# Fewer tiling changes in a fused attention and MoE kernel: three score units per visit, sums in one PSUM bank, pieces in the freed score slots

## Chip, cores and metric

One core of one Trainium2 chip. The metric is the device time of one execution in microseconds (us), the median of several. A profile's span is some 1.8 us shorter than the time of the same execution (338.66 against 336.9 for the kernel before). A run is called slow when it is over 1.5% above the fastest of its kernel; ratios use fast runs alone.

## The reference

```python
def _attn_ref(q, k, v):                 # (8, 12, 448, 64): batch, heads, sequence, head size
    scores = scale * np.matmul(q, k.transpose(0, 1, 3, 2))
    m = np.max(scores, axis=-1, keepdims=True)
    e = np.exp(scores - m)
    attn = e / (np.sum(e, axis=-1, keepdims=True) + np.exp(-m) + 1e-09)
    return np.matmul(attn, v)

def _moe_ref(x, w1, w2, w3, w_out):     # x (3584, 768); all weights (768, 768)
    h = np.maximum(np.maximum(x @ w1, x @ w2), x @ w3)
    return h @ w_out
# x is the attention's output as (8*448, 12*64)
```

## The kernel before

The work comes in 24 groups (a batch and two pairs of heads). A group has seven **score units** (four corners of 64x64 tiles, 448 columns each; they fill a two-bank PSUM slot of which three exist) and two **sums** (exponentials times v, one per pair of heads: 26 small 64x64 matmuls and 18 wide 128x128 ones). Between them TensorE does **pieces** of the projections: "up" pieces of six 448-column matmuls and "out" pieces of six 384-column ones, each in one of two further PSUM banks. A **visit** is a stretch in which TensorE leaves the pieces, changes to 64x64 tiles for scores and small sums, and comes back.

```python
visits = ((0, 1), (2, 3), (4, 5, 6))            # three visits for each group
for i in range(3, NI):
    ...
    for vi, units in enumerate(visits):
        scores(i, ej, units)                     # slots of ps_s (3 x 2 banks), exponentials on ScalarE
        if vi < 2:
            finish = av(i - 1, pj, vi, ...)      # sums of the group before, also in a slot of ps_s
        ...
        fill(per)                                # pieces, in banks of ps_b (2 x 1 bank)

def av(i, ej, pr, part):
    if i >= LAST:                                # from group 6 on
        av_tail(i, ej, pr, (0, 1, 2))            # 12 small sums, row tile r in bank r
        av_last(i, ej, pr)                       # 14 small sums of the last window
        return av_main(i, ej, pr, (0, 1, 2), True)   # 18 wide sums, then VectorE, ScalarE

def up_piece(b, fcs, i, q0, qn):
    p_i = ps_b.tile([128, 512], FP32, tag="b", name="p_i")
    # 6 matmuls with xT[b], then VectorE: hT = max(hT, p_i)

# the last tile's stores, out of add_out
cuts = [(0, NW, (sy, sy)), (NW, 256, (sc, sc)), (NW + 256, 128, (sy, sc))]
```

The softmax here doesn't subtract the row's maximum and nothing guards it: scores larger than these inputs give would overflow.

## Time and profile before

| | kernel before |
|---|---|
| time, median of 3 | 338.64 us (338.59 to 338.93) |
| span of the profile | 336.9 us |
| last matmul starts, by the trace | 331.38 us |
| tail, from there to the end | 5.50 us |
| normal visit of two units with sums | 1.394 us |

The prediction below reads the busy table, the chain, the waits and a timeline. Two more views: first the groups of instructions (line, engine, operation, out<-in, shapes, count | busy us, mean ns of one | idle before it and who ended that):

```profile
L490 PE MATMUL p_i<-xT,w 128*128 128x448 f16 (+2 forms) x972 | 173.1, 332 | 0.5 <-DMA xT<-xn 0.3
L324 ACT ACTIVATE e<-stp 128x896 f16<-128x896 f32 (+4 forms) x171 | 143.9, 901 | 60.3 <-PE stp L304 60.1
```

The pieces (L490) are half of the span and hardly ever wait. The exponentials (L324) are long, 0.9 us each, but ScalarE is idle 60 us for want of scores: here nobody on TensorE waits for it. Then the end of the timeline (start us, length us, engine, line, operation; SPq and ACTq are the sequencers of SyncE and ScalarE that issue DMAs):

```profile
330.10 3.88 SPq L531 DMA_DIRECT2D out_dram<-o_sb  x5
330.29 1.31 PE L514 MATMUL op_ps<-w,hT 128*128 128x256 f16 x12
...
331.60 1.84 ACTq L531 DMA_DIRECT2D out_dram<-o_sb  x3
```

The last store is issued on SyncE until 333.98, 2.6 us after the last matmul's start; the change tries to shorten that.

### The profile page before, as it was taken

The numbers are of one execution on the slowest core, as the hardware profiler recorded it, in microseconds if no ns is written. First come the engines' busy times: TensorE is split into PE (matmuls) and PEld (weight loads), VectorE is DVE, ScalarE is ACT, GpSimd is POOL, SyncE is SP. The second block draws the span as 40 slices with busy tenths as digits, with TensorE's granted clock in tenths as the row PEclk, the third lists the DMA queues.
The fourth block names the chain that finished last, engine by engine and source line by source line (L and its number), as shares of the span: only waits on it lengthen the run. The fifth ranks groups of instructions, "written<-read, shape, count | busy, mean of one in ns | idle before, by whom it ended". The sixth has DMA issues, their size and how long they took to land.

```text
span 336.9 us, 10248 instructions
## 1 busy us (share of the span) xinstructions
PE 326.1 (97%) x4316; PEld 195.9 (58%) x4316; DVE 199.9 (59%) x521; ACT 183.1 (54%) x289; POOL 146.7 (44%) x260
## 2 busy tenths in 40 slices
PE   7899999999999999999999999999999999999993
PEld 3668788866556655565546646555556555565552
DVE  4556675566566556556656556556556556575552
ACT  4768856655665755676556655666565665420000
POOL 8596578880671539170854328351754000000000
PEclk9999999999999999999999999999999999999999
DMA  8999999799799999969996999989990730124016
GB/s 141 197 200 207 203 205 191 128 161 191 109 108 132 171 234 145 124 96 190 177 156 81 114 259 120 150 99 220 186 149 18 164 89 2 31 47 129 0 33 157
DMA packets 84815, 46.46 MB, mean 138 GB/s; under 512 B 53280, under 2 KB 81312, under 8 KB 84768
## 3 DMA queue, kind: packets, MB, share of 16 engines
q0 software_dynamic: 29120, 21.80, 48.6%
q1 hardware_dynamic: 55264, 23.60, 41.3%
q8 instruction: 34, 0.56, 0.7%
q10 hardware_dynamic: 384, 0.39, 0.4%
q14 instruction: 13, 0.11, 0.1%
HBM read 44.04 MB, written 11.01 MB: 163 GB/s over the span
## 4 chain that ended last, share of the span: by engine, by line
PE 87%; DMA 5%; ACT 2%; DVE 2%; issue 1%; POOL 1%; POOLq 0%; ACTq 0%
PE p_i L490 48%; PE op_ps L514 14%; PE stp L304 11%; PE avp L388 9%; DMA xT<-xn 3%; ACT e L324 2%; DMA ld_q<-in_q_dram 2%; PE avp L344 2%; PE avp L361 1%; DVE xn L404 1%; PE trT L229 1%; DVE QT L190 1%; PE xtp L463 0%; ACT QT L188 0%; DVE rb L401 0%
## 5 line engine op out<-in xcount | busy, mean ns | idle before, releaser
L324 ACT ACTIVATE e<-stp 128x896 f16<-128x896 f32 (+4 forms) x171 | 143.9, 901 | 60.3 <-PE stp L304 60.1
L490 PE MATMUL p_i<-xT,w 128*128 128x448 f16 (+2 forms) x972 | 173.1, 332 | 0.5 <-DMA xT<-xn 0.3
L490 PEld LDWEIGHTS <-w 128*128 128x128 f16 x972 | 90.2, 98 | 69.1 <-issue 6.0
L249 POOL COPY QT<-QT 64x384 f16<-64x384 f16 (+1 forms) x84 | 46.9, 558 | 93.9 <-DMA QT<-ld_q 69.2
L501 DVE TENSOR_TENSOR hT<-hT,p_i 128x448 f16<-128x448 f16 (+2 forms) x96 | 59.7, 622 | 35.7 <-PE p_i L490 35.6
L514 PE MATMUL op_ps<-w,hT 128*128 128x384 f16 (+2 forms) x342 | 58.5, 323 | 0.0
L304 PE MATMUL stp<-QT,KT 64*64 64x448 f16 (+2 forms) x756 | 48.1, 338 | 2.6 <-ACT e L324 0.9
L499 DVE CAST hT<-p_i 128x448 f16<-128x448 f32 (+2 forms) x48 | 30.0, 625 | 25.2 <-PE p_i L490 25.2
L514 PEld LDWEIGHTS <-hT 128*128 128x128 f16 x342 | 32.0, 98 | 22.4 <-issue 2.0
L424 ACT ACTIVATE xn<-end,rl 64x64 f16<-64x64 f32 x72 | 24.9, 346 | 34.5 <-DVE rl L421 34.1
L521 DVE TENSOR_SCALAR o_sb<-op_ps 128x384 f32<-128x384 f32 (+2 forms) x57 | 31.2, 547 | 17.4 <-PE op_ps L514 16.8
L388 PE MATMUL avp<-vx,e 128*128 128x65 f16 x936 | 38.6, 194 | 0.0
L388 PEld LDWEIGHTS <-e 128*128 128x128 f16 x936 | 32.1, 97 | 2.3
L304 PEld LDWEIGHTS <-KT 64*64 64x64 f16 x756 | 15.8, 105 | 26.8 <-issue 23.9
L398 DVE TENSOR_SCALAR rb<-avp 128x6 f32<-128x6 f32 (+2 forms) x54 | 8.8, 164 | 36.8 <-PE avp L388 36.8
L404 DVE TENSOR_TENSOR xn<-avp,rb 128x384 f16<-128x384 f32 (+2 forms) x54 | 29.3, 543 | 1.8
L433 POOL COPY vx<-ld_v 128x768 f16<-128x768 f16 x21 | 17.2, 820 | 6.8 <-issue 4.2
L344 PEld LDWEIGHTS <-e 64*64 64x64 f16 x624 | 13.7, 107 | 8.1 <-issue 1.7
L102 POOL DMA_DIRECT2D ld_q<-in_q_dram x24 | 17.4, 723 | 2.3 <-DMA w<-in_moe_w_dram 1.1
L102 POOL DMA_DIRECT2D ld_k<-in_k_dram x24 | 17.3, 722 | 2.1 <-DMA w<-in_moe_w_out_dram 1.1
L414 ACT ACTIVATE end<-avp 128x65 f32<-128x65 f32 x36 | 8.2, 227 | 17.1 <-PE p_i L490 12.4
L115 POOL DMA_DIRECT2D ld_v<-in_v_dram x24 | 15.2, 634 | 2.6 <-DMA w<-in_moe_w_dram 1.3
(52 smaller groups left out, 162.1 us busy)
## 6 DMA issues: line engine op xcount, KB each, us to landing
out_dram<-o_sb SPq DMA_DIRECT2D x54, 192.0 KB, 4.0
ld_v<-in_v_dram POOLq DMA_DIRECT2D x48, 128.0 KB, 5.1
ld_k<-in_k_dram POOLq DMA_DIRECT2D x23, 224.0 KB, 6.6
ld_q<-in_q_dram POOLq DMA_DIRECT2D x23, 224.0 KB, 7.5
w<-in_moe_w_dram POOLq DMA_DIRECT2D x9, 384.0 KB, 9.2
w<-in_moe_w_out_dram POOLq DMA_DIRECT2D x3, 384.0 KB, 8.5
xT<-xn SPq DMA_TRANSPOSE x18, 4.8
QT<-ld_q SPq DMA_TRANSPOSE x17, 7.3
```

The source lines that it names most:

```text
L102: nc.gpsimd.dma_start(out=tiles[nm][:, 1 : NP * T + 1].rearrange("x (r t) d -> x r (t d)", r=NP)[:, p0:p1], in_=src[:, p0:p1],)
L249: eng.tensor_copy(out=t[d0 : d0 + HP, o * 128 : (o + n) * 128], in_=t[s0 : s0 + HP, a * 128 : (a + n) * 128],)
L304: nc.tensor.matmul(out=stp[half * HP : half * HP + HP, par, j * qn : (j + 1) * qn], lhsT=k_block(i, pr, h2, x[half]), rhs=q_cols(i, pr, h2 ...
L324: nc.scalar.activation(out=dst, in_=src, func=AF.Exp, scale=scale)
L388: nc.tensor.matmul(out=ps[:, hh, j * D1 : (j + 1) * D1], lhsT=eF[:, o : o + 128], rhs=vx[:, 2 * pr + hh, (x[0]), 0:D1], start=False, stop= ...
L404: nc.vector.tensor_tensor(out=xn[i][:, pr, ws[0] : ws[0] + nw].rearrange("p j h d -> p h j d"), in0=acc[:, :, :, 0:D], in1=rb.unsqueeze(3) ...
L424: nc.scalar.activation(out=xn[i][0:HP, pr, 3, hh], in_=end[h, 0:D], func=AF.Copy, scale=rl[h])
L490: nc.tensor.matmul(out=p_i[:, j * qn : (j + 1) * qn], lhsT=w_sb[i][:, dc, ts(fc, 128)], rhs=xT[b][:, dc, q0 : q0 + qn], start=(dc == 0), s ...
L499: nc.vector.tensor_copy(out=dst, in_=src)
L501: nc.vector.tensor_tensor(out=dst, in0=dst, in1=src, op=ALU.max)
L514: nc.tensor.matmul(out=op_ps[:, 0:w], lhsT=hT[bp][:, fc, ts(t, 128)], rhs=wout_sb[:, fc, c : c + w], start=(fc == 0), stop=(fc == NFC - 1),)
L521: nc.vector.tensor_scalar(out=o_sb[:, c : c + w], in0=op_ps[:, 0:w], scalar1=1.0 / LAMBDA, scalar2=None, op0=ALU.mult,)
```

## The change

The intent: fewer changes of tiling. From group 6 on, three groups (21 units) take seven visits of three units instead of nine visits of two or three. That needs PSUM: the sums move out of the slots into one bank that is always the same, and the pieces of a visit go into the score slots as their exponentials empty them, the last one into the other bank. The order of the corners, and a no-op on ScalarE, keep small sums of two row tiles from writing one bank at once. xT (the transposed attention output) of one group more, the last of batch 1, comes by DMA and not from TensorE. The last stores go on three queues. The core of the diff, cuts marked:

```diff
+    slots = [ps.tile([128, 2, 512], FP32, name=f"ps{j}") for j in range(3)]
+    banks = [ps.tile([128, 512], FP32, name=f"pb{j}") for j in range(2)]
 ...
+    def visit(units, pair):
 ...
+        ps = banks[0]                            # the sums, always here
 ...
+            for at in anti:
+                s0(*at)
+            turned = turn_over(smalls(diag, True))
+            for s, at in ((s0, diag), (s1, anti), (s1, diag), (s2, anti), (s2, diag)):
+                for corner in at:
+                    s(*corner)
+            smalls(anti, False, turned)
+            for _, power in qk:
+                power()                          # three exponentials on ScalarE
+            wides()
 ...
-                cuts = [(0, NW, (sy, sy)), (NW, 256, (sc, sc)), (NW + 256, 128, (sy, sc))]
+                cuts = [(0, NW, (sy, sc)), (NW, 256, (gp, gp)), (NW + 256, 128, (sy, sc))]
 ...
+    def places(cols, pair):                      # where the n pieces of this visit go
 ...
+        mid = [] if pair else [banks[0]]
+        while len(mid) < n:
+            mid.append(slots[(turn["s"] + len(mid) - (not pair)) % 3][:, 0])
+        ahead.extend(mid[: max(n - 1, 0)] + [banks[1]] * (n > 0))
 ...
+    for g in range(ONE, NI, 3):                  # ONE = 6
+        todo = [(g + n // 7, n % 7) for n in range(21)]
+        for n in range(7):
+            us = todo[3 * n : 3 * n + 3]
 ...
+            if pr == 1:
+                x_transpose_dma(pi)
```

## The prediction

> **What bounds the kernel now.** I read the page's busy table and clock row first, then the chain that ended last, then the waits of TensorE, and last a timeline of TensorE alone over three visits. The busy table:
>
> ```profile
> PE 326.1 (97%) x4316; PEld 195.9 (58%) x4316; DVE 199.9 (59%) x521; ACT 183.1 (54%) x289; POOL 146.7 (44%) x260
> PEclk9999999999999999999999999999999999999999
> ```
>
> Only TensorE (PE) is full, at full clock in every slice. Busy is not yet proof, so the chain and the waits (columns: engine and line, waited for: us in total, times, longest us):
>
> ```profile
> PE 87%; DMA 5%; ACT 2%; DVE 2%; issue 1%; POOL 1%; POOLq 0%; ACTq 0%
> ...
> PE stp L304 <- ACT e L324: 0.9, 3, 0.4
> ...
> PE p_i L490 <- DMA xT<-xn: 0.3, 1, 0.3
> ...
> PEld L304 <- issue: 23.9, 74, 0.6
> ```
>
> The chain is TensorE for 87%. It waits hardly at all for another engine: 0.9 us for exponentials (in the first 40 us) and 0.3 us for one transposed xT. What stands out is the last row: 74 times the weight loader sits idle 0.32 us before a run of scores and waits for nothing. That is a cost of changing from 128x128 to 64x64 tiles. Three visits of one group (start us, length us, engine, line):
>
> ```profile
> 149.55 0.65 PE L514 MATMUL op_ps<-w,hT 128*128 128x384 f16 x3
> 150.13 0.57 PE L304 MATMUL stp<-QT,KT 64*64 64x448 f16 x8
> 150.53 0.26 PE L344 MATMUL avp<-vt,e 64*64 64x65 f16 x12
> ...
> 150.85 0.73 PE L388 MATMUL avp<-vx,e 128*128 128x65 f16 x18
> 151.43 2.11 PE L514 MATMUL op_ps<-w,hT 128*128 128x384 f16 x12
> ...
> 154.77 3.56 PE L490 MATMUL p_i<-xT,w 128*128 128x448 f16 x18
> 158.27 0.76 PE L304 MATMUL stp<-QT,KT 64*64 64x448 f16 x12
> 158.96 0.36 PE L490 MATMUL p_i<-xT,w 128*128 128x448 f16 x1
> ```
>
> Pieces (the up and out projections) run at a fixed pitch: the 18 matmuls take 3.56 us of which the last is about 0.35, so 3.21/17 = 0.189 us each; the 384-column ones 0.162 us. The pieces are already at full rate, so time can only come out of what lies between them. I measure that as (first piece after) minus (start of the last piece before plus one pitch). A visit of two score units and sums: 149.55 + 3 x 0.162 = 150.03 to 151.43 = 1.40 us. A visit of three units without sums: 154.77 + 18 x 0.189 = 158.17 to 158.96 = 0.79 us. By the trace's start stamps, the 1.394 of a normal visit is 0.094 change of tiling, 0.40 scores (2 quads of four concurrent 64x64 matmuls, about 0.2 each), 0.32 for 26 small sums (about 31 ns per four) and the change back, and 0.575 for 18 wide sums (32 ns each). The change back alone is about 0.1: a last score quad takes 0.29 us to the next piece instead of 0.19.
>
> **What the Trainium skill says.** "TensorEngine Tiling (Array Packing)", Key Properties: changing the tiling mode drains TensorE. The trace agrees: 0.094 us in and about 0.1 us out per visit. "PSUM — Partial Sum Buffer", PSUM bank collisions: two TensorE writes from different row tiles into one bank and quadrant collide. The kernel before keeps row tile r in bank r, as that asks; no run here tests it. It explains the change's order of corners and its turn-over through ScalarE. "ScalarE: Activation LUTs", What ACT_TABLE_LOAD costs: an activation with immediates takes 186 ns + 0.833 ns per column, 93 ns of it overlapped back to back. For 896 columns that is an estimate of 932, then 839; the trace has 917 and a pitch of 0.80 to 0.81. "DMA: Bandwidth & Descriptors", Issuing engines are not separate DMA queues: another issuing engine saves only the sequencer's time. In the tail of the trace that time is real: the last SyncE issues are 0.5 to 0.9 us each, in series.
>
> **The change, part by part.**
>
> 1. Fewer visits. From group 6 on, 54 visits (and two more for the last sums) become 42 and one. Sums are also moved into visits with three units: 37 of the 42 carry sums (one pair is left for the end), 5 are scores alone. Matmul counts stay at 4316 by the built program's order, so only changes of tiling and waits can differ.
>
> 2. One visit with three units and sums, if nothing waits. The two anti corners of unit 0 start at 0.094. The 14 diagonal small sums run beside them on the other two tiles, 7 per tile at about 31 ns, to 0.315. Then unit 0's diagonal corners at 0.315, unit 1 at 0.505, unit 2 at 0.694 (pitch 0.189). The 12 anti small sums run beside the end of unit 2. Wide sums start at 0.694 + 0.29 = 0.985 and end at 1.56. So the third unit costs about 0.17 where a visit of its own would add two changes of tiling. The no-op on ScalarE is ready near 0.6, before the anti sums want it at 0.69; I count nothing for it.
>
> 3. The new wait. In 36 of the 37 visits the first piece goes into the score slot of unit 0 and must wait for its exponential (the built order has a wait on ScalarE there; in one visit the only piece goes to the bank). Unit 0 is complete only at 0.315 + 0.355 (a later quad's matmul is 0.349) = 0.67; ScalarE starts 0.052 after (before: quad ends at 0.383, exponential starts at 0.435) and needs 0.917, so 1.64; TensorE starts 0.051 after an ACT end (same in every such wait before). First piece at 1.69, not 1.56: **a wait of 0.13 us in each of 36 visits**, 4.7 us. Second and third pieces (at 2.8, 4.0; or 2.7, 3.6 for out pieces) come after exponentials that end at 2.45 and 3.25: no wait. The next visit's slots were emptied long before.
>
> 4. Sum from group 6 on. Before: 34 x 1.394 + 17 x 0.788 + group 6's three (1.485 + 1.488 + 1.246, still with PE transposes of xT) + 2 x 1.018 at the end = 67.06 us. After: 36 x 1.69 + 1.56 + 5 x 0.79 + 1.33 for the last sums alone (1.02 and 0.3 for two more changes of tiling and slower pairs of small tiles) = 67.68 us. **+0.6 us**. Without the wait it would be 63.0, or -4.1 us: the wait eats the gain.
>
> 5. Off the path. ScalarE loses 36 x (0.23 + 2 x 0.35) = 33 us, VectorE swaps four small operations for two scalings. Neither is the bound (54% and 59%), so nothing.
>
> 6. xT by DMA. Before, one transfer of 9.54 us held TensorE 0.46 us. The new lead at a batch's start is about 11 us (two visits of 5.5 and one of 1.7, less 2.3 for VectorE), the slowest issue-to-landing before was 10.2: that stall may go. Batch 1's lead is only about 8 us, as the visits there have one or two pieces: maybe 0.3. At the end, four out pieces (3.9 us) cover a transfer that takes about 4.7 from the last sum: 0.1 after the first four matmuls. Net -0.1.
>
> 7. Tail. Last matmul starts at 331.38, last SyncE issue 333.51 to 333.98, landed 335.60. With one issue of the wide cut on SyncE, one on ScalarE and the middle cut on GpSimd, SyncE's last issue is some 1.2 us earlier, but GpSimd issues take 0.63 to 0.72 each and then travel: landing near 335.1 to 335.2. -0.4 us.
>
> 338.64 + 0.6 - 0.1 - 0.4 = 338.7. The pitch of small tiles in pairs may be 30 and not 31 ns; seven of them then start unit 0's diagonal corners 7 ns sooner, 0.25 us over 36 visits. I take it off: **338.4 us**.
>
> **The rivals.** (a) The gain comes whole: the first piece finds its slot free. Then 36 x 0.13 = 4.7 less, about 334. For it: nothing in TensorE's order forces the stall but that one wait. Against it: the exponential's start and length repeat to some 2 ns in the trace before. (b) The small sums do not run beside the scores on the other tiles. All four tiles running at once before (score quads 1.6 ns apart in issue) speaks against it, but mixed lengths in flight were never seen. It would add up to 0.19 us x 37 = 7 us: 345. (c) The turn-over through ScalarE is late, because the no-op queues behind exponentials of a short visit. ScalarE needs 2.5 of 5.4 us, so only in the first three visits: below 1 us. (d) xT arrives late, as its DMA now starts nearer to the bursts of loads after a group: 1 us per late batch, up to 3.
>
> **Range and chances.** (a) to (d) put the time between 334 and 345, most weight on 337 to 340. I take 334.5 to 341.5 for 8 in 10. 2% is 6.8 us: faster needs more than the whole gain of part 4 (0.03); slower needs (b) in full (0.06); within, 0.91.
>
> **What would show it.** In the profile after: tiling changes before scores fall from 74 to about 62 (54 visits become 42); a row of TensorE pieces waiting for the exponentials of about 36 times 0.13 us (right if 3 to 6 us in all, and then ACT's share of the chain grows); visits with sums take 1.69 (if 1.56, rival a; if 1.85 or more, b or c); small sums start within 10 ns of unit 0's anti corners; pieces keep 0.189; the last landing is about 3.6 us after the last matmul, not 4.2. The prediction is wrong if scores and small sums exclude each other on the array, or if unit 0's exponential can be done by 1.5.

## The result, and the profile after

**349.78 us**, median of 4 runs (348.55 to 378.87), against 338.62 (338.24 to 338.93, 4 runs) for the kernel before: ratio 1.0318, 95% interval 1.0266 to 1.037, slower. A ratio is the mean time of one kernel's fast runs over that of the other's of the same rounds, so not quite the ratio of the medians quoted. The run of 378.87 us had a granted clock of 0.85 (its trace shows 0.85 without a change from 5.5 to 374.1 us); it was the first one, none of the later runs showed it again, and its cause is open. Its profile is not used: the profile "after" below is of a second series of the unaltered kernel, 347.67 us (346.35 to 351.82, 6 runs) against 340.01 (337.78 to 342.94, 11 runs), ratio 1.0228 [1.0165, 1.0291]: still slower, but whether by more than 2% this series leaves unclear.

The busy table and the clock row of the page after:

```profile
PE 330.5 (96%) x4316; PEld 202.8 (59%) x4316; DVE 201.6 (58%) x488; ACT 149.8 (43%) x181; POOL 147.6 (43%) x262
...
PEclk9999999999999999999999999999999999999998
```

TensorE is still the only full engine, with the same 4316 matmuls. ScalarE lost 33.3 us of work (183.1 to 149.8), as predicted, and it brought nothing, as predicted. The waits (engine and line, waited for: us in total, times, longest):

```profile
ACT e L425 <- PE ps L414: 110.2, 37, 5.6
...
PEld L414 <- issue: 14.5, 42, 0.4
...
PEld L322 <- issue: 5.9, 21, 0.7
...
PE ps L594 <- DMA xT<-xn: 1.7, 1, 1.7
```

The tiling changes before scores fell from 74 to 42 + 21 = 63 (predicted: about 62). One wait for xT is longer than before. But the row that the prediction wanted, TensorE pieces waiting some 36 times for exponentials, is not there. Nobody may conclude from this that the wait is not. A normal visit with three units and sums, in the timeline of TensorE:

```profile
92.94 0.38 PE L414 MATMUL ps<-QT,KT 64*64 64x448 f16 x2
92.94 0.31 PE L452 MATMUL pb<-vt,e 64*64 64x65 f16 x8
93.09 0.23 PE L452 MATMUL pb<-vx,e 64*64 64x65 f16 x4
93.15 0.35 PE L414 MATMUL ps<-QT,KT 64*64 64x448 f16 x2
93.16 0.19 PE L452 MATMUL pb<-vx,e 64*64 64x65 f16 x2
93.19 0.54 PE L414 MATMUL ps<-QT,KT 64*64 64x448 f16 x6
...
93.85 0.74 PE L481 MATMUL pb<-vx,e 128*128 128x65 f16 x18
94.58 3.57 PE L594 MATMUL ps<-xT,w 128*128 128x448 f16 x18
```

And in the timeline of ScalarE, same window:

```profile
93.61 2.54 ACT L425 ACTIVATE e<-ps 128x896 f16<-128x896 f32 x3 [3.74 <-PE ps L414]
```

Three exponentials take 2.54 us, each about 0.917 (the mean of L425 is 918 ns), so unit 0's ends near 93.61 + 0.917 = 94.53. The first piece (94.58) starts 0.05 later. The 18 wide sums start at 93.85 and have a pitch of 32 ns: they are issued by 93.85 + 18 x 0.032 = 94.43, which is when a piece could have started. So TensorE stands for 0.15 us. The waits view misses it because the record of a wide sum lasts 0.19 us: the last one, started near 94.39, is drawn until 94.58 and covers the gap. Stalls shorter than the record of one instruction show only in start stamps.

Adding up start stamps over the trace (what lies between the last piece's pitch and the next piece, as in the prediction) splits the span of both profiles:

| us | predicted change | before | after | change |
|---|---|---|---|---|
| first stretch of pieces ends (it starts at 22.54 and 22.32) | 0 | 23.67 | 23.45 | -0.22 |
| between pieces, before group 6 | 0 | 21.80 | 22.00 | +0.20 |
| between pieces, from group 6 | +0.35 | 67.09 | 70.98 | +3.89 |
| gaps from one piece to the next | -0.1 | 1.58 | 5.00 | +3.42 |
| tail | -0.4 | 5.50 | 7.06 | +1.56 |
| span | -0.15 | 336.88 | 345.64 | +8.76 |

(The parts sum to 8.85; 0.1 is unassigned.) Three places are wrong, and each got experiments.

### The profile page after: what moved, and what is told of

It is laid out like the page before. It is cut to its first block, busy times and chain, and to the rows that moved or that the text cites. A ratio compares the mean times of both kernels' runs of the same rounds, so it can differ in the third digit from the quotient of the medians.

```text
span 377.0 us, 10297 instructions
## 1 busy us (share of the span) xinstructions
PE 364.1 (97%) x4316; PEld 215.0 (57%) x4316; DVE 202.2 (54%) x488; ACT 150.0 (40%) x181; POOL 148.0 (39%) x262
## 4 chain that ended last, share of the span: by engine, by line
PE 94%; DVE 2%; ACT 2%; issue 1%; POOL 0%; POOLq 0%; DVEq 0%; ACTq 0%
PE ps L594 28%; PE pb L594 22%; PE pb L618 8%; PE ps L618 8%; PE ps L414 7%; PE pb L481 7%; PE pb L452 3%; PE ps L322 2%; PE ps L379 2%; ACT e L342 1%; PE pb L195 1%; PE pb L247 1%; PE ps L362 1%; DVE QT L210 0%; PE ps L231 0%
## 5 line engine op out<-in xcount | busy, mean ns | idle before, releaser
L425 ACT ACTIVATE e<-ps 128x896 f16<-128x896 f32 x126 | 106.5, 917 | 149.2 <-PE ps L414 128.3
L594 PE MATMUL ps<-xT,w 128*128 128x448 f16 x480 | 109.8, 387 | 0.2 <-ACT e L425 0.2
L594 PE MATMUL pb<-xT,w 128*128 128x448 f16 (+2 forms) x492 | 91.6, 341 | 0.7 <-DVE o_sb L625 0.6
L605 DVE TENSOR_TENSOR hT<-hT,ps 128x448 f16<-128x448 f16 x59 | 36.6, 621 | 21.6 <-PE ps L594 12.8
L342 ACT ACTIVATE e<-ps 128x896 f16<-128x896 f32 (+4 forms) x45 | 36.5, 869 | 21.0 <-PE ps L322 19.3
L414 PE MATMUL ps<-QT,KT 64*64 64x448 f16 x504 | 44.0, 382 | 0.0
L618 PE MATMUL pb<-w,hT 128*128 128x384 f16 (+2 forms) x180 | 36.6, 350 | 0.0
L605 DVE TENSOR_TENSOR hT<-hT,pb 128x448 f16<-128x448 f16 (+2 forms) x37 | 23.0, 621 | 23.0 <-PE pb L594 23.0
L618 PE MATMUL ps<-w,hT 128*128 128x384 f16 x162 | 32.4, 358 | 0.0
L481 PE MATMUL pb<-vx,e 128*128 128x65 f16 x684 | 28.4, 195 | 0.0
```

The costliest lines, as they stand in the source:

```text
L342: nc.scalar.activation(out=dst, in_=src, func=AF.Exp, scale=scale)
L414: return nc.tensor.matmul(out=stp[half * HP : half * HP + HP, par, 0:S], lhsT=k_block(i, pr, h2, x[half]), rhs=q_cols(i, pr, h2, par, "EO" ...
L425: nc.scalar.activation(out=dst, in_=stp[:, :, 0:S], func=AF.Exp, scale=scale)
L481: nc.tensor.matmul(out=ps[:, (3 * hh + j) * D1 : (3 * hh + j + 1) * D1], lhsT=eF[:, o : o + 128], rhs=vx[:, 2 * pr + hh, (x[0]), 0:D1], st ...
L594: nc.tensor.matmul(out=p_i[:, j * qn : (j + 1) * qn], lhsT=w_sb[i][:, dc, ts(fc, 128)], rhs=xT[b][:, dc, q0 : q0 + qn], start=(dc == 0), s ...
L605: nc.vector.tensor_tensor(out=dst, in0=dst, in1=src, op=ALU.max)
```

## The experiments

The theory: (W) the first piece waits for unit 0's exponential, 0.15 us in each of some 36 visits; (X) the xT of group 5, wanted at batch 1's start, lands too late; (B) one bank for pieces collides where two pieces follow at a batch's change, and one bank for sums collides in short visits; (S) late stores on GpSimd lengthen the tail. The rivals: the visits are longer for another reason (small sums do not run beside scores), the gaps come from slower DMA in general, and the tail is only the last data's landing.

### The kernel unaltered, once more (after_again)

> The changed kernel, unaltered, to get a profile in the fast state (its first profile fell in a state with a granted clock of 0.85, 377 us). Theory W (the new wait of the first piece on unit 0's exponential, as drawn in the prediction): visits with sums take 1.69 us, the wait in all is about 4.7 us, and the time is 338 to 340 us; then the measured 348.6 is not explained by it. Theory C (clock): pieces keep a pitch of 0.189 us at a granted clock of 1.00, but the clock is granted below 1.00 in stretches even in runs called fast, which shows as pitches of about 0.218 us; 8 us more would need a mean clock near 0.975. Theory S (a stall somewhere that the prediction did not see, for instance a late transfer of xT or slots not yet emptied): a few long gaps of TensorE, together about 8 us, at full clock.

Measured: the series and the profile above, and the first table. It settles which terms are wrong. The small sums start 6 ns after unit 0's first corners in a normal visit (both 92.94 in the timeline above): they do run beside scores, so that rival falls. Nor is DMA slower in general: the median time of an xT transfer from issue to landing is 4.8 us in both profiles.

### Only the last stores (stores_only)

```diff
 # the kernel before, with this alone (and gp = nc.gpsimd)
-                cuts = [(0, NW, (sy, sy)), (NW, 256, (sc, sc)), (NW + 256, 128, (sy, sc))]
+                cuts = [(0, NW, (sy, sc)), (NW, 256, (gp, gp)), (NW + 256, 128, (sy, sc))]
```

> The kernel before with only the last three stores spread over three queues as in the change. Prediction's part 7: last landing about 0.4 us earlier, time 338.2 us, ratio 0.999. If the GpSimd queue is slower than thought, the last landing moves later by up to 2 us (340.5 us), and part of the 10 us lies there.

Measured: 340.58 us (339.71 to 342.22, 6 runs), ratio 1.0021 [0.9971, 1.0071]: the times cannot tell 1.5 us. The profile can: its tail is 7.02 us instead of 5.50. The timeline after, at the end:

```profile
337.82 2.33 SPq L635 DMA_DIRECT2D out_dram<-o_sb  x3
337.82 0.98 PE L618 MATMUL pb<-w,hT 128*128 128x256 f16 x9
...
338.29 1.35 ACTq L635 DMA_DIRECT2D out_dram<-o_sb  x2
...
339.07 1.11 POOL L635 DMA_DIRECT2D out_dram<-o_sb  x2 [73.74 <-DVE o_sb L625]
```

SyncE's last issue does end 1 us sooner (1.56 us after the last matmul's start at 338.58, not 2.60), and the last data land after 3.93 us, not 4.22. Yet the program ends later. The trace's records say why (start and end, us from the last matmul's start; cut):

```
+0.49 +1.05  POOL DMA_DIRECT2D   landed +3.01
+1.04 +1.60  POOL DMA_DIRECT2D   landed +3.74
+1.03 +1.56  SP   DMA_DIRECT2D   landed +3.93
+0.94 +6.24  POOL DRAIN
+4.44 +4.45  SP   DRAIN
```

SyncE is done waiting at +4.45. GpSimd's closing drain ends only at +6.24, 4.6 us after its last issue and 2.5 us after that issue's data landed; what remains of the program's end comes after it.

### GpSimd stores one tile earlier (gp_one_tile_earlier)

```diff
 # the kernel before, last stores as before
+            if b == B - 1 and t == 5:
+                cuts = [(0, NW, None), (NW, NW, (gp, gp))]
```

> The kernel before with the stores of the last tile but one issued by GpSimd, and nothing else moved: GpSimd's last issue is some 2 us sooner than in the run with the last stores spread over three queues. There its closing drain lasted from 0.94 to 6.24 us after the last matmul's start, although its last data had landed at 3.84, and it alone held the program's end (7.0 us after the last matmul and not 5.5). Theory D1 (the drain ends some 4.6 us after GpSimd's last issue, whatever else goes on): it ends at about 3 to 4 us here and costs nothing, tail 5.5 us. Theory D2 (the drain of a GpSimd that has issued late waits for something at the program's end, and ends at 6.2 whenever it issued): tail 7.0 us again.

Measured: 339.89 us in one run; GpSimd's last issue ended at +0.10, its data landed at +2.94, the drain ended at +5.28, and the tail was 6.06. So the drain ended 5.2 us after the last issue here and 4.6 after it above: neither theory fits whole. The drain moves with GpSimd's last store, but not one for one: an issue 1.5 us earlier saved 0.96 of the 1.52 us, and even this one cost about 0.6. Why the drain takes so long is not shown.

### The changed kernel with the old stores (stores_undone)

```diff
-                cuts = [(0, NW, (sy, sc)), (NW, 256, (gp, gp)), (NW + 256, 128, (sy, sc))]
+                cuts = [(0, NW, (sy, sy)), (NW, 256, (sc, sc)), (NW + 256, 128, (sy, sc))]
```

> The changed kernel with only the last stores put back as in the kernel before. Theory D (the two late GpSimd issues cost 1.5 us, by GpSimd's closing drain): the tail after the last matmul falls from 7.06 to 5.5 us and the time by 1.5 us, to about 346. Rival (the tail depends on what else ran): tail stays above 6.5 us.

Measured: 347.4 us (346.87 to 348.6, 4 runs), ratio 1.024 [1.0182, 1.0298]. The tail is 5.06 us, 2.0 less than after, and the time did not follow. Its last matmul started 2.2 us later, at 340.81. The timeline at batch 1's start says where that came from:

```profile
80.30 0.92 PE L594 MATMUL ps<-xT,w 128*128 128x448 f16 x4
83.13 3.21 PE L594 MATMUL ps<-xT,w 128*128 128x448 f16 x9 [1.92 <-DMA xT<-xn]
```

After a stall of 2.08 us (by start stamps) nine matmuls came 373 ns apart instead of 189: 9 x 0.184 = 1.66 us more. This is the next point.

### Pieces begin and end in the piece bank (bank_ends)

The first piece takes the free piece bank and only the second goes to unit 0's slot, where three or more pieces follow a visit with sums.

```diff
-        mid = [] if pair else [banks[0]]
+        mid = [banks[1]] if pair and n > 2 else [] if pair else [banks[0]]
+        first = len(mid)
         while len(mid) < n:
-            mid.append(slots[(turn["s"] + len(mid) - (not pair)) % 3][:, 0])
+            mid.append(slots[(turn["s"] + len(mid) - first) % 3][:, 0])
```

> The changed kernel with one thing moved: in a visit with sums and three or more pieces the first piece goes into the piece bank (free since the visit before) as well as the last, and only those between go into score slots. Theory W (the first piece waits for unit 0's exponential, 0.15 us in each of some 33 visits): a visit with sums falls from 1.737 to 1.585 us, the span by 33 x 0.15 = 5.0 us, and the rest stays. Rival R (the visit of 1.737 is TensorE's own, from sharing the array; the piece would start no sooner in another bank): visits stay at 1.73 and the time within 1 us. Rival V (the last piece now waits for the first one's evacuation from the same bank, as VectorE also has the sums to take out): visits fall but gaps between pieces of 0.1 us or more take the gain back.

Measured: the time between pieces from group 6 fell from 70.98 to 65.65 us, by 5.33, and the normal visit from 1.737 to 1.586. The timeline of one:

```profile
92.08 0.58 PE L414 MATMUL ps<-QT,KT 64*64 64x448 f16 x8
...
92.78 0.73 PE L481 MATMUL pb<-vx,e 128*128 128x65 f16 x18
93.35 1.29 PE L594 MATMUL pb<-xT,w 128*128 128x448 f16 x6
94.48 2.43 PE L594 MATMUL ps<-xT,w 128*128 128x448 f16 x12
```

From the wide sums' start to the first piece it is 93.35 - 92.78 = 0.57 us, 18 pitches of 32 ns, where it was 0.73 after. The six matmuls that now come first write pb, a bank; those of the slot (ps) come 1.13 us later, when the exponential is long done. **W is shown**: same matmuls, only the place of the first piece differs.

The time did not show the whole of it: 345.46 us (342.1 to 347.33, 4 runs). Two runs were fast (343.61, 342.1), ratio 1.0092 [1.0046, 1.0138], and two slow, one of them profiled:

```profile
80.26 0.92 PE L594 MATMUL pb<-xT,w 128*128 128x448 f16 x4
86.03 0.90 PE L594 MATMUL pb<-xT,w 128*128 128x448 f16 x2 [4.86 <-DMA xT<-xn]
86.73 4.07 PE L594 MATMUL ps<-xT,w 128*128 128x448 f16 x12
```

The wait for xT was 5.02 us by start stamps, and nine of the matmuls after it came 373 ns apart, with two more between the two rates, 1.95 us lost in all; (4.07 - 0.35)/11 = 0.34 is the mean pitch of the last twelve. The view by windows (from and to, length, busy us of each engine, then PEclk, the granted clock, DMA share and GB/s) has for this stretch:

```profile
77.00:83.00 6.00, 4.17 (x70) 2.52 (x69) 3.01 (x8) 3.53 (x5) 0.64 (x3) 1.00 1.88 93
83.00:87.00 4.00, 0.97 (x3) 0.40 (x3) 0.03 (x1) 0.00 (x0) 0.00 (x0) 0.53 1.09 173
87.00:91.00 4.00, 4.00 (x14) 1.67 (x13) 1.80 (x5) 0.00 (x0) 1.84 (x4) 0.62 1.09 205
91.00:95.00 4.00, 4.00 (x70) 2.49 (x69) 2.38 (x6) 2.46 (x3) 3.96 (x7) 1.00 1.00 121
```

The clock goes from 1.00 to 0.53 and 0.62 and back; TensorE, busy all of 87 to 91, does 14 matmuls where at full clock 21 fit (4.00/0.189). The Trainium skill, "TensorE: Matmul & The Clock Gate", Part 1, gives this: after an idle window of about 3.4 us TensorE runs at half clock until it has been busy for one. This trace agrees in kind (189 to 373 ns is half). The clock records in the traces tell more. In every profile each stretch at one clock, from the first change to the last, lasts a whole number of 3.413 us: 23 x 3.413 = 78.51, 2 x 3.413 = 6.83 (the half clock here, from 83.20 to 90.03) and 74 x 3.413 = 252.59 in bank_ends, 1 x 3.413 in stores_undone (83.49 to 86.90), 96 x 3.413 = 327.68 in all_four. So the clock changed only at the edges of windows of fixed length, and it fits the traces that the idle time within one window decides. Here is an estimate of that, with each matmul taken as busy for one pitch from its start stamp. The window before the half clock was idle for 2.20 us both in stores_undone and here. The profile after had 2.07 us (the wait and the short gaps around it) in the window that ended at 82.78 and kept the full clock; in end_bank an edge at 81.77 split the wait between two windows, and neither had more than 1.6. The same count over all windows of the 13 profiles in which full clock was granted puts every window of 2.07 us or less before full clock and every one of 2.20 or more before half clock. That is less than the whole idle window of the page. Where the edges fall differs from run to run, so part of this loss is luck.

### xT of group 5 on TensorE (x5_on_pe)

```diff
-            if pr == 1:
+            if pr == 1 and pi >= ONE:
                 x_transpose_dma(pi)
 ...
+        if n == NV0 + 2:
+            ahead.append(banks[1])
+            x_transpose_all(ONE - 1)
```

> The changed kernel with group 5's xT transposed on TensorE again, as before, in the visit before batch 1 starts. Theory X (the transfer of group 5, 8.15 us from issue to landing, holds batch 1's first piece for 1.85 us, because the visits in front of it hold one or two pieces only): the wait of TensorE for the transfer of xT goes, eight transposes of about 0.46 us come, span 1.4 us less. Rival: another wait stands right behind it (ScalarE or VectorE's copy of xT) and the span stays within 0.5 us.

Measured: 346.63 us in one run. The wait for xT is gone, gaps between pieces fall from 5.00 to 3.49, and the last matmul starts at 337.42, 1.16 sooner, though the first piece came 0.31 later. The span fell by only 0.78 of the 1.4 us expected, as the tail was 0.4 longer in this run. X is shown at its place, by one run. In the timeline after, at the same place:

```profile
80.18 0.92 PE L594 MATMUL ps<-xT,w 128*128 128x448 f16 x4
82.79 2.81 PE L594 MATMUL ps<-xT,w 128*128 128x448 f16 x14 [1.69 <-DMA xT<-xn]
```

That DMA was issued at 74.60 and landed at 82.745, 8.15 us later; the piece wanted it at 80.9, a lead of 6.3 us. It was 1.85 us late there, 2.05 in end_bank, 2.08 in stores_undone and 5.02 in bank_ends, where the transfer took 11.2 us. The transfer's length varies from run to run, and no run here was made to say with what. One hint: in before, after, bank_ends, stores_undone and end_bank the transfers of xT issued from 265 us on, when the last loads of q, k and v had landed, took 3.0 to 3.4 us, those issued earlier 3.0 to 11.2.

### The piece banks swapped before the last batch (end_bank)

At the last batch's start the two banks met. The timeline after:

```profile
308.38 1.14 PE L618 MATMUL pb<-w,hT 128*128 128x384 f16 x6
...
309.56 0.56 DVE L625 TENSOR_SCALAR o_sb<-pb 128x384 f32<-128x384 f32 x1 [0.42 <-PE pb L618]
310.17 2.05 PE L594 MATMUL pb<-xT,w 128*128 128x448 f16 x10 [0.65 <-DVE o_sb L625]
```

The last out piece sits in a bank until VectorE has emptied it at 310.12; the first up piece of the last batch gets the same bank and starts at 310.17, 0.81 us late by start stamps.

```diff
     fill(float("inf"))
+    turn["b"] += 1
     add_batch(B - 1)
```

> The changed kernel with the two banks swapped once after the last sums, so that the last batch's first piece does not get the bank that the out piece just in front of it used. Theory E (the 0.81 us gap at 310.2 us is the wait for VectorE to empty that same bank): the gap falls to 0.1 us or less, span 0.75 us less. Rival: the transfer of the last group's xT, which landed at 310.14, holds TensorE then anyway, four matmuls later (0.76 us), and the gap only moves: span within 0.2 us.

Measured: 348.01 us in one run. The first up piece now follows the out piece without a gap, and its fifth matmul waits 0.07 us for the transfer: 0.07 instead of 0.81. The sum of gaps was 5.11 and not 4.3: this run had two waits for xT, 2.05 and 0.66 us. A miss in the time, a hit at the place.

### All four mends (all_four, all_four_again)

bank_ends, x5_on_pe, end_bank and the old stores together.

> The changed kernel with four parts mended at once: pieces begin and end in the bank, group 5's xT on TensorE, the banks swapped before the last batch, the last stores as in the kernel before. If the four costs are what the trace of the changed kernel shows (5.0, 1.4, 0.75 and 1.5 us) and add up: 8.6 us less than the changed kernel, 339.0 us, within 0.5% of the kernel before, and what is left over the drawn gain of 3 us are the waits of small sums for the single bank in the first short visits (1.2 us) and the slower small tiles (36 and not 31 ns). If a cause is still missing, it stays above 341.

Measured: 338.53 us (338.43 to 338.88, 4 runs), ratio 0.9967 [0.9942, 0.9992]. Once more with five rounds:

> The four mends together, unaltered, with five rounds instead of three, because 0.9967 [0.9942, 0.9992] in the first series barely excludes 1. Theory: 338.5 us, ratio 0.997, interval below 1. Rival: the first interval was luck and the ratio is 0.998 to 1.001.

Measured: 338.7 us (338.08 to 339.91, 6 runs), ratio 0.9971 [0.9939, 1.0004]. The four mends account for the loss: the span falls from 345.6 to 336.8 and 336.5, with 65.68 us between pieces from group 6, gaps of 2.69 and 2.50 and a tail of 5.48 and 5.41. Whether the result beats the kernel before by 0.3% the second interval just does not say.

### Pieces held back for the short visits (early_8_two_queues, early_5_two_queues, early_8)

The prediction hoped for 63.0 us without the wait, and 65.7 came. Most of the rest lies in three visits at 70 to 80 us that had one or two pieces each and took 2.42, 2.01 and 2.00 us. In the timeline after:

```profile
69.95 0.38 PE L414 MATMUL ps<-QT,KT 64*64 64x448 f16 x2
...
69.99 0.57 DVE L523 TENSOR_SCALAR xn<-pb,rb 64x64 f16<-64x64 f32 x2
...
70.61 0.31 PE L452 MATMUL pb<-vt,e 64*64 64x65 f16 x8 [0.29 <-DVE xn L523]
```

The small sums should start with the scores, at 69.95. They start at 70.61, because VectorE reads the sums of the visit before out of the one bank until 69.99 + 0.57 = 70.56: 0.66 us lost, and 0.30 in each of the next two. So pieces are held back before group 6 and dealt out evenly over the first three visits (their pieces are then 3.26, 1.95 and 1.95 us long, not 0.97, 1.95 and 1.95; with factor 0.5, 3.93, 2.92 and 2.92). Two of the three runs also have the last stores alternate between SyncE and ScalarE.

```diff
-        per = STEP if n < 2 else share(n)
+        per = STEP if n < 2 else share(n) * (0.8 if n < NV0 else 1.0)    # or 0.5
+        if NV0 <= n < NV0 + 3:
+            credit[0] = 0.0
+            per = sum(w for _, _, w in pieces[: -(-len(pieces) // (NV0 + 3 - n))]) - 1.0
 # the two-queue runs
-                cuts = [(0, NW, (sy, sy)), (NW, 256, (sc, sc)), (NW + 256, 128, (sy, sc))]
+                cuts = [(0, NW, (sy, sc)), (NW, 256, (sc, sy)), (NW + 256, 128, (sy, sc))]
```

> The kernel with all four parts mended, and two more things: one out piece is held back from the visits before group 6 for the first visits with three units (3.26, 1.95, 1.95 us of pieces there and not 0.97, 1.95, 1.95), and the last three stores alternate over SyncE and ScalarE alone. Theory B (in those first visits the small sums wait for VectorE to empty the one bank of sums, 1.2 us in all, because too few pieces lie between): the wait falls to about 0.5 us, span 0.7 us less; last landing about 0.3 us sooner. 337.5 us, ratio to the kernel before 0.994. Rival: the visits before group 6, with less to do, wait for ScalarE or VectorE instead, and nothing is won.

Measured: 338.34 us (338.2 to 338.43, 4 runs), ratio 0.9969 [0.9928, 1.0009]. Between pieces from group 6: 64.95 us, 0.73 less; the last matmul 1.05 us sooner than in all_four (330.25); but the tail is 6.09 instead of 5.48.

> As the other of this pair, with more held back: 3.93, 2.92, 2.92 us of pieces in the first three visits with three units. Theory B: no small sum waits for the bank of sums any more, visits there take 1.59 to 1.74, span 1.2 us less than with all four parts mended: 337.0 us. Rival: the visits before group 6, of which one now has no piece at all, wait for exponentials and lose 0.5 us or more.

Measured: 338.57 us (338.38 to 339.22, 4 runs), ratio 0.9979 [0.9937, 1.0022]. From group 6 64.25, but before it 24.42 instead of 21.99: one of the earlier visits now has no piece at all, and the time held back there was lost there. The two queues brought nothing in either run (tails 6.09 and 5.62).

> All four mends, plus the credit held back before group 6 (0.8 of the share) so that the first three visits of the new plan get pieces enough to keep their sums away from the one bank; last stores as in the kernel before. In the two-queue version this brought the last matmul from 331.30 to 330.25 us, but its tail was 6.09 us instead of 5.48. Theory: the credit and the stores are independent, so span 330.25 + 5.5 = 335.7, time 337.6, ratio to the kernel before 0.995 (about 0.3% under all_four of the same call). Rival: the 0.6 us of tail came from the earlier end itself (the stores then fall on other transfers), so span 336.3 and time 338.3, no different from all_four.

Measured: **338.02 us** (337.43 to 338.31, 6 runs), ratio 0.9947 [0.9916, 0.9979], beside 338.7 for all_four_again in the same series on the same chip. The span is 335.7, the last matmul starts at 330.10, the tail is 5.56: the theory's numbers, and the rival (a tail that lengthens because the end comes earlier) falls. The page:

```profile
PE 324.9 (97%) x4324; PEld 201.1 (60%) x4324; DVE 202.8 (60%) x489; ACT 149.9 (45%) x181; POOL 146.6 (44%) x260
```

TensorE is 1.2 us less busy than before the change, in spite of eight more matmuls (the transposes of xT). This version beats the kernel before by 0.5% in its own series (the interval excludes 1), and the changed kernel by some 3% across series (338.02 against 347.67).

## Why the prediction was wrong

It said 338.4 us, between 334.5 and 341.5, and within 2%; the kernel took 349.78 and in the second series 347.67, outside the range. Three of its steps failed. Part 4 was 3.3 us short, since the one bank of sums makes short visits wait and the wait for the exponential is longer than drawn. Part 6 said -0.1 us for gaps and +3.42 came, for the lead of a transfer and a piece bank at the last seam. Part 7 said -0.4 for the tail and +1.56 came, by GpSimd's drain. (Two slips in its sums are small: 338.74 - 0.25 is 338.5 and not 338.4, and two visits of 5.5 and one of 1.7 less 2.3 are a lead of 10.4 and not 11.) By its own steps:

1. **Fewer visits: right.** 63 tiling changes before scores, about 62 predicted.
2. **A visit without the wait, 1.56: nearly right.** It is 1.586 (the one visit after whose only piece goes to the bank, at 67.30, shows 1.585). The step assumed 31 ns for small tiles; in pairs they have 36 (the first pair at 0.100, the seventh at 0.316 after the last piece: 0.216/6). Unit 0's diagonal corners start at 0.348 and not 0.315. The step at the end of part 4, which took 0.25 us off because the pitch might be 30, went the wrong way.
3. **The new wait: mechanism right, size too small.** The visit takes 1.737 and not 1.69, as the exponential starts later by those 33 ns and a little; the wait is 0.152 and not 0.13. Over some 33 visits that is 33 x 0.047 = 1.55 us of the 3.3 us that part 4 is short. bank_ends shows the wait as a cause: 5.33 us came back.
4. **"The next visit's slots were emptied long before": the step that failed here.** True of slots, but not of the one bank of sums, which the prediction never examined. In the three short visits it cost 0.66 + 0.30 + 0.30; they exceed the 1.69 by 0.73, 0.32 and 0.31, together 1.36 us. One further visit was 0.28 longer than the rest (2.016), and the last sums 0.08. 1.55 + 1.36 + 0.33 + 0.08 = 3.32, against 70.98 - 67.68 = 3.30 measured.
5. **Off the path: right.** ScalarE lost 33 us and nothing moved.
6. **xT by DMA, "Net -0.1": failed.** Batch 1's stall was sized at "maybe 0.3" and was 1.85 to 5.02, with 1.66 and 1.95 us of half clock behind it in two profiles. The term that was mis-sized is the lead: "about 8 us" predicted, 6.3 measured (74.60 to 80.9). With 8 us, the transfer of 8.15 would have cost 0.15. That a transfer can take longer (11.2 in bank_ends) was there to be read, as the prediction had seen 10.2. The later leads were shorter than drawn, too: 9.0 us in end_bank (150.12 to 159.1), where a transfer of 9.6 cost 0.66. At the end, 0.1 was predicted and 0.81 came, since a bank and not the transfer ended the wait (the first four matmuls want an xT that had landed at 299.0; end_bank, without the bank's wait, shows the transfer's own part, 0.07). With smaller waits for hT these make the +3.42 us of gaps.
7. **Tail, -0.4: failed in sign.** The landing was as predicted (3.93 after the last matmul, where 3.6 was said); what ends the program is GpSimd's drain, which the step did not know. +1.56 us. stores_only, gp_one_tile_earlier and stores_undone show it.

Of the rivals, (a) fell; (b) fell by the 6 ns between scores and small sums; (c), a late no-op, appeared in no stamp of a normal visit; (d) happened in one batch: 1.85 us in the profile after, and with the half clock 3.7 in stores_undone and 7.0 in bank_ends, past its upper end of 3. The prediction weighed four rivals as alternatives. What came was several small losses added, each of the same sign: 1.6 for the wait and pitches, 1.4 for the bank, 3.4 for gaps, 2.0 against its gain for the tail. The test "a row of about 36 waits" was the wrong test for a stall of 0.15 us, as shown above.

Open: the first run's clock of 0.85; what makes the transfer of xT take 8 or 11 us (the loads are a suspect, not tested); why GpSimd's drain takes about 5 us; and what follows the 0.2 us before group 6.

## What to carry to other kernels

When buffers are shared anew, write down for each one who empties it last and when it is wanted next, in the shortest visit and at every seam and not only in the normal visit: all losses here but the exponential's wait and the slower small tiles came at a seam. Let the first work after a burst write where nothing must be emptied first, and let what depends on the burst come second; this swap alone was worth 5.3 us of 345. Measure stalls by start stamps where an instruction's record is longer than the stall, and keep late stores off GpSimd when its closing drain would end the program.

## What the Trainium skill lacked or had wrong

- "DMA: Bandwidth & Descriptors", Issuing engines are not separate DMA queues: that another engine saves only sequencer time leaves out the program's end. GpSimd's closing drain ended 4.6 to 5.2 us after its last store was issued, 2.3 to 2.5 us after that store's data had landed, and the tail grew from 5.50 to 7.02 us.
- "TensorE: Matmul & The Clock Gate", Part 3, The mechanism: it states that matmuls start in strict program order. The stamps here do not: in program order (that of kernel.py) all 14 small sums come before any corner but unit 0's first two, and unit 0's diagonal corners before unit 1's, yet a pair of corners starts at 0.307 us, ahead of the last two small sums (0.316) and of unit 0's diagonal corners (0.348), which are on other tiles. The line at 93.15 shows it ahead of the one at 93.16.
- The same page, Part 1: half clock after an idle window of about 3.4 us. Here 2.20 us of idle time in a window of 3.413 us (estimated from start stamps, as shown above) was followed by half clock, and 2.07 us was not.
- "TensorEngine Tiling (Array Packing)", Instruction Overhead: it names a least cost of a matmul but no pitch for rounds of small ones. Here a round of 65-column matmuls on two tiles took 36 ns, beside scores on the other two, and one on all four took 31 ns.
- "Perfetto Trace Analysis", Tensor Engine Instruction (MATMUL, LD_WEIGHTS): it says that a matmul's end in a profile is computed and not observed, but does not warn what follows for waits. Here the record of a short matmul (0.19 us for 65 columns at a pitch of 32 ns) hid a wait of 0.15 us from the view of waits.
